# Second MLP's tiles 1 and 2: seven half-size block products for each two f-blocks

## The chip, the cores and the metric

The kernel runs on one core of one Trainium2 chip. The metric is device time in microseconds of one execution on that core, median of several runs. The kernel before takes 796.52 us (median of three: 794.61, 796.52, 796.79).

## What is computed

Clustered attention over 2 x 8 heads of 768 positions and 64 channels, and then two MLPs on the 1536 x 512 result. The change lies in the second MLP's first product, `x @ w_in`.

```python
def _moe_ref(x, w_in, w_out):            # first MLP, 512 -> 2048 -> 512
    h = x @ w_in
    g = h * np.cos(h)
    return (g @ w_out).astype(np.float32)

def _moe2_ref(x, w_in, w_out):           # second MLP, 512 -> 2048 -> 512
    h = x @ w_in
    g = np.where(h > 0.0, h, 1.0 * (np.exp(np.minimum(h, 0.0)) - 1.0))
    return (g @ w_out).astype(np.float32)
```

## The kernel before

The 1536 tokens are cut into three tiles of 512 (`t`), the 2048 inner columns into 16 f-blocks of 128 (`f`). `SEQ` lists the 96 steps (m, t, f): MLP m, tile t, block f. Every fp32 operand is held as two fp32r parts, a rounded high part and the rest (XH/XL of the activations in `X`, the two halves of a weight's slot, GH/GL of the inner result), and a product is three matmuls: high x high, high x low, low x high.

- `g1` (line 203) makes h of one step: 4 blocks of the contraction (kd) x 3 matmuls = 12 matmuls with 128 x 128 weights and 512 moving columns, summed in one PSUM bank (`ps_h`, 4 banks).
- `act` makes g of it: in the second MLP Relu and Exp on ACT (lines 236, 238), one operation on DVE (240), the copy GH (line 82 when on ACT) and the rest GL (245).
- `g2` (line 262) adds g's part of the output: 4 x 3 matmuls of 512 columns into four PSUM banks (`ps_a`), which stay for the 16 steps of a tile. `finish` copies them out at the tile's end.
- `x_hi`, `x_lo` (line 184) split a tile's x into XH, XL. `load_w` and `w_part` fetch the 16 slots of a MLP's weights and split them. For the second MLP the split goes on during its tile 0; tiles 1 and 2 only read the slots.

No engine's order is left to chance: every call goes into a list with a time in steps (tables `FIRST`, `PAIR`, `STEP`, ..., `LAST`, `MLP`), the list is sorted by it, and that is each engine's order of instructions. A step's `g1` in the second MLP stands at 1.6, its `g2` at 5.7, so `g2` runs about four steps behind. The table `OWN` and its like say which engine does an operation that several can do. `xpl` holds, in the attention stage, two kinds of buffers (R and xt, line 829 and 846) of three each.

Of the kernel before, what the change touches and what calls it, by code (L numbers as in the profile page):

```python
# [1015 lines left out]
```

## Time and profile before

| | |
|---|---|
| median of three runs | 796.52 us |
| the profiled execution, own time | 799.22 us |
| its span, first to last instruction | 797.4 us |
| TensorE matmul busy | 778.0 us (98%) |
| TensorE weight loads busy | 670.1 us (84%) |
| DVE, ACT, POOL busy | 507.9, 472.9, 329.3 us (64, 59, 41%) |
| granted TensorE clock, mean | 0.996 |

The attention stage takes the first 267 us, the first MLP goes to about 529 us, and the second MLP's three tiles take some 87 to 90 us each. A matmul's record (389 ns for 512 columns) is longer than the distance from one to the next, since matmuls are pipelined; it is the distance between starts that counts. Weight loads have records of their own (PEld) beside them. The records of the merged timeline give a start, the time to the end of the last instruction that they hold, and their number.

### The profile page before, as it was taken

The page shows a single profiled execution, that of the slowest core. Times are in us where ns is not written, and L with a number is a line of the kernel's source. Part 1 is how long each engine was busy: PE and PEld are TensorE (multiplying, and loading weights), DVE is VectorE, ACT ScalarE, POOL GpSimd, SP SyncE. Part 2 cuts the span into 40 slices and gives each one's busy share as a digit, 9 for nine tenths or more (in the row PEclk, how much of TensorE's full clock was granted, in tenths as well). Part 3 has the DMA queues.
Part 4 walks back from the last instruction along what each step waited for, and adds up shares of the span by engine and source line. Part 5 has one row for each costly group of instructions (what it writes and reads, how often), then busy time and mean ns, then how long its engine had stood idle before and what let it go on. Part 6 is the DMA issues. An engine that isn't in the chain of part 4 may idle for free.

```text
span 797.4 us, 11263 instructions
## 1 busy us (share of the span) xinstructions
PE 778.0 (98%) x4003; PEld 670.1 (84%) x4003; DVE 507.9 (64%) x791; ACT 472.9 (59%) x887; POOL 329.3 (41%) x419
## 2 busy tenths in 40 slices
PE   6999999999999999999999999999999999999998
PEld 5888998989898888888888888888888888888886
DVE  7899899999999999964545555997773111112110
ACT  5888998988989866743434434655452433334323
POOL 6666666766765633132321222256440122113211
PEclk9899999999999999999999999999999999999999
DMA  4637556548447395000000055643000100000001
GB/s 101 154 71 163 137 122 161 129 96 194 91 113 251 46 379 186 1 1 0 1 1 0 8 175 188 211 159 106 0 1 1 53 1 1 0 27 27 0 1 53
DMA packets 62919, 67.98 MB, mean 85 GB/s; under 512 B 30416, under 2 KB 51408, under 8 KB 62864
## 3 DMA queue, kind: packets, MB, share of 16 engines
q1 hardware_dynamic: 62864, 67.28, 30.2%
q8 instruction: 31, 0.51, 0.3%
q14 instruction: 24, 0.20, 0.1%
HBM read 46.17 MB, written 3.19 MB: 62 GB/s over the span
## 4 chain that ended last, share of the span: by engine, by line
PE 89%; DVE 7%; DMA 1%; ACT 1%; issue 0%; ACTq 0%
PE h L203 33%; PE a L262 33%; PE pt L774 7%; PE px L805 6%; PE s L751 4%; PE s L754 3%; PE pt_sim L586 2%; DVE m L759 2%; DVE PL L794 2%; DVE M L652 1%; PE pt_raw L445 1%; DMA row<-sum 1%; PE pt_mask L661 1%; ACT P L765 0%; DVE best L638 0%
## 5 line engine op out<-in xcount | busy, mean ns | idle before, releaser
L203 PE MATMUL h<-XH,slot 128*128 128x512 f32 x768 | 249.6, 389 | 0.0
L245 POOL TENSOR_TENSOR GL<-A,GH 128x512 fp32r<-128x512 f32 x77 | 104.3, 1355 | 285.4 <-ACT GH L82 275.3
L203 PEld LDWEIGHTS h<-XH,slot 128*128 128x128 f32 x768 | 144.2, 188 | 29.8
L203 PE MATMUL h<-XL,slot 128*128 128x512 f32 x384 | 149.4, 389 | 0.0
L262 PE MATMUL a<-GH,slot 128*128 128x512 f32 x384 | 124.2, 389 | 0.0
L240 DVE SCALAR_TENSOR_TENSOR A<-R,h 128x512 f32<-128x512 f32 x48 | 32.9, 685 | 136.7 <-ACT R L238 110.5
L262 PE MATMUL a<-slot,GH 128*128 128x512 f32 x384 | 118.1, 389 | 0.0
L794 DVE TENSOR_TENSOR PL<-pt,PH 128x384 fp32r<-128x384 f32 x192 | 99.8, 548 | 13.2 <-ACT PH L788 12.0
L759 DVE TENSOR_REDUCE m<-s 128x1 f32<-128x768 f32 x96 | 91.3, 951 | 3.0 <-PE s L754 2.8
L788 ACT ACTIVATE PH<-pt 128x384 fp32r<-128x384 f32 x192 | 84.0, 495 | 14.2 <-PE pt L774 13.9
L765 ACT ACTIVATE P<-s,m 128x768 f32<-128x768 f32 x96 | 87.2, 909 | 0.2
L262 PEld LDWEIGHTS a<-GH,slot 128*128 128x128 f32 x384 | 72.1, 188 | 15.1
L774 PE MATMUL pt<-ident,P 128*128 128x128 f32 x576 | 83.9, 280 | 0.8 <-DVE PL L794 0.8
L262 PEld LDWEIGHTS a<-slot,GH 128*128 128x128 f32 x384 | 72.1, 188 | 14.9
L203 PEld LDWEIGHTS h<-XL,slot 128*128 128x128 f32 x384 | 72.1, 188 | 14.8
L262 PE MATMUL a<-GL,slot 128*128 128x512 f32 x192 | 74.7, 389 | 0.0
L262 PE MATMUL a<-slot,GL 128*128 128x512 f32 x192 | 74.7, 389 | 0.0
L774 PEld LDWEIGHTS pt<-ident,P 128*128 128x128 f32 x576 | 66.8, 142 | 7.5 <-DVE PL L794 2.6
L82 ACT ACTIVATE GH<-A 128x512 fp32r<-128x512 f32 x74 | 46.5, 628 | 43.1 <-PE a L262 35.0
L236 ACT ACTIVATE R<-h 128x512 f32<-128x512 f32 x48 | 28.4, 593 | 67.8 <-PE h L203 59.3
L232 ACT ACTIVATE R<-R,cbias 128x512 f32<-128x512 f32 x48 | 34.8, 724 | 51.8 <-DVE R L229 51.5
L805 PE MATMUL px<-PH,V 128*128 128x384 f32 x192 | 63.8, 360 | 0.2 <-issue 0.2
(148 smaller groups left out, 1281.3 us busy)
## 6 DMA issues: line engine op xcount, KB each, us to landing
raw<-in_moe_w_in_dram SPq DMA_DIRECT2D x32, 512.0 KB, 4.9
raw<-in_moe_w_out_dram SPq DMA_DIRECT2D x32, 512.0 KB, 5.6
nat_k<-in_k_dram SPq DMA_DIRECT2D x16, 192.0 KB, 4.9
nat_q<-in_q_dram SPq DMA_DIRECT2D x16, 192.0 KB, 4.8
nat_v<-in_v_dram SPq DMA_DIRECT2D x8, 384.0 KB, 4.2
R<-row SPq DMA_DIRECT2D x32, 96.0 KB, 3.4
out_dram<-o SPq DMA_DIRECT2D x12, 256.0 KB, 2.0
X0k<-hi SPq DMA_DIRECT2D x7, 192.0 KB, 3.2
```

Source lines behind the costliest of these rows:

```text
L82: nc.scalar.activation(out=out, in_=in_, func=AF.Copy)
L203: nc.tensor.matmul(h, lhsT=a[:, kd, :], rhs=b, start=(kd == 0 and i == 0), stop=(kd == NKD - 1 and i == 2))
L232: nc.scalar.activation(out=R, in_=R, func=AF.Sin, scale=-2.0 * PI, bias=cbias[:, 1:2])
L240: nc.vector.scalar_tensor_tensor(out=A, in0=R, scalar=-1.0, in1=h, op0=ALU.add, op1=ALU.max)
L245: eng.tensor_tensor(out=GL, in0=A, in1=f32(GH), op=ALU.subtract)
L262: nc.tensor.matmul(accs[m, t][e], lhsT=a, rhs=b, start=(f == 0 and i == 0), stop=(f == NF - 1 and i == 2))
L759: nc.vector.tensor_reduce(out=m, in_=st[n]["s"][:, :, 0:HW], axis=AX.XY, op=ALU.max, negate=True)
L765: nc.scalar.activation(out=P, in_=st[n]["s"][:, :, 0:HW], func=AF.Exp, bias=st[n]["m"], accum_out=den_all[:, u % NDEN, j, r, 0:1])
L774: nc.tensor.transpose(pt[:, c * 128:(c + 1) * 128], st[n]["P"][:, e, c * 128:(c + 1) * 128], ident)
L788: nc.scalar.activation(out=ph, in_=pt, func=AF.Copy)
L794: nc.vector.tensor_tensor(out=pl, in0=pt, in1=f32(ph), op=ALU.subtract)
L805: nc.tensor.matmul(tx[g][:, 0:HW], lhsT=V2s[pp][:, j, c, :], rhs=halves[g][a][:, c, :], start=(n == 0), stop=(n == 2 * C - 1))
```

## The change

For tiles 1 and 2 of the second MLP, two f-blocks form a pair p (f = 2p and 2p+1). The weights of the pair are cut into four blocks of 256 contraction rows x 128 inner columns: A11, A12 are the two contraction halves of f = 2p+1, A21, A22 those of f = 2p. The tile's x is cut into four blocks of 256 contraction rows x 256 tokens, B11, B12, B21, B22. Instead of eight block products (24 matmuls of 512 columns for the pair) seven are formed, from sums of blocks: S1 to S4 of the A, T1 to T4 of the B. Each product (`prod`) is 2 contraction blocks x 3 matmuls of 256 columns, 42 matmuls for a pair, into half a PSUM bank.

- `s_u`, `s_one`, `s_two` add and split the S of each pair, S1 in tile 1 alone (it replaces A21 in the slot). S2 to S4 lie in one pair of tiles (`s_tiles`) that all pairs share.
- `b_sum`, `b_hi`, `b_lo` add and split the T and B once for each tile (table `WB`).
- `post` adds the products to the two blocks of h, in SBUF instead of PSUM; `act2` does what `act` did, from there.
- The table `WINO` orders all of it in pairs of steps. The tables `MLP` and `OWN` are new numbers throughout; the first copy of one head's keys (`HI2_ON['k', 1]`) goes from ACT to POOL; R and xt become slices of one tile `XR`, taken in turn by three as before, whose place the parts of B21, B22 and T2 take later.

```diff
@@ tables (MLP and OWN are replaced as a whole; the entries that the text speaks of) @@
-MLP = ({'g1': 1.9351, 'g2': 5.1777, 'load_w': 6.9247,
...
-        {'w_part:0': -2.691, 'g1': 1.6453, 'g2': 5.685, 'finish:0': 5.1595,
...
+MLP = ({'g1': 2.0325, 'g2': 5.796, 'load_w': 8.7032,
...
+        {'w_part:0': -1.5449, 'g1': 1.3739, 'g2': 5.8639, 'finish:0': 6.1734,
...
-OWN = {('whi', 0, 4): 'act', ('whi', 0, 5): 'pool',
...
+OWN = {('whi', 0, 4): 'dve', ('whi', 0, 5): 'dve',
...
+WINO = {'prod:0': 1.6, 'prod:1': 1.9725, 'prod:2': 2.6787, 'prod:3': 2.7425, 'prod:4': 2.7906, 'prod:5': 1.7613, 'prod:6': 3.234, 's_u:0': 0.9693, 's_u:1': 0.8845, 's_one:0': 1.3791, 's_one:1': 1.6966, 's_one:2': 2.1605, 's_two:0': 1.4297, 's_two:1': 1.5803, 's_two:2': 1.7361, 's_two:3': 2.1336, 's_two:4': 1.7614, 's_two:5': 2.2728, 'post:0': 2.7063, 'post:1': 2.7432, 'post:2': 3.0948, 'post:3': 3.2081, 'post:4': 3.2392, 'post:5': 3.6463, 'act2:0:0': 3.4126, 'act2:0:1': 3.4277, 'act2:0:2': 3.4505, 'act2:0:3': 3.4527, 'act2:0:4': 4.0437, 'act2:1:0': 4.1999, 'act2:1:1': 4.2131, 'act2:1:2': 4.3675, 'act2:1:3': 4.809, 'act2:1:4': 4.9979, 'g2:0': 4.8891, 'g2:1': 5.7143, 'finish:0': 6.1536, 'finish:1': 6.3053, 'finish:2': 6.3697, 'finish:3': 6.9415}
+WB = {1: {'b_sum:T3': -12.515, 'b_sum:T1': -8.3378, 'b_hi:B22': -12.3147, 'b_lo:B22': -8.8721, 'b_sum:T2': -4.6837, 'b_hi:B21': -10.5531, 'b_lo:B21': -10.0989, 'b_sum:T4': -0.1752, 'b_hi:T2': 0.3261, 'b_lo:T2': 0.3985, 'b_hi:B11': 0.0969, 'b_lo:B11': 1.4943, 'b_hi:T1': 0.9416, 'b_lo:T1': 2.25, 'b_hi:T3': 2.2503, 'b_lo:T3': 2.2727, 'b_hi:T4': 1.4624, 'b_lo:T4': 2.1361}, 2: {'b_sum:T3': -5.1851, 'b_sum:T1': -10.2681, 'b_sum:T2': -10.1178, 'b_sum:T4': -8.5532, 'b_hi:B11': 0.297, 'b_lo:B11': 0.439, 'b_hi:T2': 0.7126, 'b_lo:T2': 0.9837, 'b_hi:T1': 1.597, 'b_lo:T1': 2.1008, 'b_hi:T3': 0.7567, 'b_lo:T3': 1.2414, 'b_hi:T4': 0.9759, 'b_lo:T4': 1.6384, 'b_hi:B21': 0.5348, 'b_lo:B21': 1.5059, 'b_hi:B22': 2.4049, 'b_lo:B22': 2.6018}}
+BSUM_ON = "pool"
+B_ON = {"B11": ("act", "dve"), "B21": ("act", "pool"), "B22": ("act", "pool"), "T1": ("act", "dve"), "T2": ("act", "dve"),
+        "T3": ("act", "dve"), "T4": ("act", "dve")}
+SU_ON = ("pool", "pool")
+SONE_ON = "dve"
+G2_ON = (("act", "pool"), ("act", "pool"))
-HI2_ON = {('k', 0): 'act', ('k', 1): 'act', ('q', 0): 'act', ('q', 1): 'act'}
+HI2_ON = {('k', 0): 'act', ('k', 1): 'pool', ('q', 0): 'act', ('q', 1): 'act'}
...
-    xpl = ctx.enter_context(tc.tile_pool(name="xpl", bufs=2))
+    xpl = ctx.enter_context(tc.tile_pool(name="xpl", bufs=1))
+    XR = xpl.tile([128, 6, HW], F32, tag="xr", name="xr")
...
+    TH = TT // 2
+    PRODS = (("11", "B11", 0, 1), ("S2", "T2", 0, 0), ("S1", "T1", 1, 1), ("S3", "T3", 1, 0), ("22", "T4", 2, 0),
+             ("12", "B21", 3, 0), ("S4", "B22", 3, 1))
+    BT, BF, hw, HA = {}, {}, {}, {}
...
+    def b_tiles(t, b):
+
+        own = {"B11": 0, "T3": 1, "T4": 2, "T1": 3}
+        if b in own:
+            if (t, b) not in BT:
+                BT[t, b] = [blk(xs_pool[0].tile([128, TT], F32R, tag=f"{n}{own[b]}", name=n)) for n in ("XH", "XL")]
+        elif (1, b) not in BT:
+            u = xpl.tile([128, 9, TH], F32R, tag="xr", name="BX")
+            top = top_pool[0].tile([128, 2, TH], F32R, name="BY")
+            BT[1, "B22"] = [u[:, 0:2], u[:, 2:4]]
+            BT[1, "B21"] = [u[:, 4:6], u[:, 6:8]]
+            BT[1, "T2"] = [top, (u[:, 8], s_tiles()[0][:, 3])]
+        return BT[t, b] if b in own else BT[1, b]
...
+    def x_block(t, b):
+        i, j = int(b[1]) - 1, int(b[2]) - 1
+        return X[:, 2 * i:2 * i + 2, t * TT + j * TH:t * TT + (j + 1) * TH]
...
+    def b_sum(t, b):
+
+        a, c, op = {"T3": ("B22", "B12", ALU.subtract), "T1": ("B12", "B11", ALU.subtract),
+                    "T2": ("B22", "T1", ALU.subtract), "T4": ("B21", "T2", ALU.subtract)}[b]
+        if t > 1:
+            home = blk(X[:, ("T1", "T2", "T3", "T4").index(b), TT:2 * TT])
+        elif b == "T3":
+            home = blk(X[:, 2, 0:TT])
+        else:
+            home = x_block(t, {"T1": "B12", "T2": "B22", "T4": "B21"}[b])
+            need(*([("b_sum", t, "T3")] if b == "T1" else [("b_lo", t, {"T2": "B22", "T4": "B21"}[b])]))
+        for x in (a, c):
+            if x[0] == "T":
+                need(("b_sum", t, x))
+            else:
+                BF[t, x] = x_block(t, x)
+        eng = nc.vector if BSUM_ON == "dve" else nc.gpsimd
+        eng.tensor_tensor(out=home, in0=BF[t, a], in1=BF[t, c], op=op)
+        BF[t, b] = home
+        made("b_sum", t, b)
...
+    def b_hi(t, b):
+        if b[0] == "T":
+            need(("b_sum", t, b))
+        else:
+            BF[t, b] = x_block(t, b)
+        for o, x in pieces(b_tiles(t, b)[0], BF[t, b]):
+            copy_on(B_ON[b][0], o, x)
+        made("b_hi", t, b)
...
+    def b_lo(t, b):
+        need(("b_hi", t, b))
+        hi, lo = b_tiles(t, b)
+        eng = nc.vector if B_ON[b][1] == "dve" else nc.gpsimd
+        for k, (o, x) in enumerate(pieces(lo, BF[t, b])):
+            eng.tensor_tensor(out=o, in0=x, in1=f32(piece(hi, k) if isinstance(lo, tuple) else hi), op=ALU.subtract)
...
+    UV = X[:, 0:2, 0:TT].rearrange("p c (e n) -> p c e n", e=2)
+    HV = X[:, 2:4, 0:TT].rearrange("p c (e n) -> p c e n", e=2)
+
+    def s_u(t, p, i):
+
+        ih, il, _, _ = w_views(1, 2 * p + 1 - i)
+        eng = nc.vector if SU_ON[i] == "dve" else nc.gpsimd
+        eng.tensor_tensor(out=X[:, i, 0:TT].rearrange("p (k f) -> p k f", k=NKD), in0=f32(ih), in1=f32(il), op=ALU.add)
...
+    def s_one(p, i):
+
+        a = UV[:, 1, 0]
+        ih, il, _, _ = w_views(1, 2 * p)
+        eng = nc.vector if SONE_ON == "dve" else nc.gpsimd
+        if i == 0:
+            eng.tensor_tensor(out=a, in0=a, in1=UV[:, 1, 1], op=ALU.add)
+        elif i == 1:
+            copy_on("act", ih[:, 0:2], k2(a))
+        else:
+            eng.tensor_tensor(out=il[:, 0:2], in0=k2(a), in1=f32(ih[:, 0:2]), op=ALU.subtract)
...
+    def s_two(t, p, i):
+        hi, lo = s_tiles()
+        if i == 0:
+            nc.vector.tensor_tensor(out=UV[:, 0, 0], in0=UV[:, 1, 0], in1=UV[:, 0, 0], op=ALU.subtract)
+        elif i == 1:
+            nc.vector.tensor_tensor(out=UV[:, :, 1], in0=UV[:, :, 1],
+                                    in1=UV[:, 0:1, 0].to_broadcast([128, 2, TH]), op=ALU.subtract)
+        else:
+            x, ks = ((UV[:, 0], slice(0, 2)), (UV[:, 1, 1:2], slice(2, 3)))[i % 2]
+            if i < 4:
+                copy_on("act", hi[:, ks], x)
+            else:
+                nc.vector.tensor_tensor(out=lo[:, ks], in0=x, in1=f32(hi[:, ks]), op=ALU.subtract)
...
+    def a_block(t, p, a):
+        if a in ("S2", "S4", "S3"):
+            i = ("S2", "S4", "S3").index(a)
+            return [x[:, i].rearrange("p (k f) -> p k f", k=2) for x in s_tiles()]
+        ih, il, _, _ = w_views(1, 2 * p + 1 if a[0] == "1" else 2 * p)
+        ks = slice(0, 2) if a in ("11", "S1") else slice(2, 4)
+        return [ih[:, ks], il[:, ks]]
...
+    def prod(t, p, i):
+        a, b, bank, half = PRODS[i]
+        need(("b_lo", t, b))
+        if a[0] == "S":
+            need(("s_one", p, 2) if a == "S1" else ("s_two", t, p, 5 if a == "S3" else 4))
+        if (t, p, bank) not in hw:
+            hw[t, p, bank] = ps_h.tile([128, TT], F32, tag="h", name="h")
+        o = hw[t, p, bank][:, half * TH:(half + 1) * TH]
+        ah, al = a_block(t, p, a)
+        bh, bl = b_tiles(t, b)
+        for k in range(2):
+            for n, (x, y) in enumerate(((ah, bh), (ah, bl), (al, bh))):
+                nc.tensor.matmul(o, lhsT=x[:, k], rhs=piece(y, k), start=(k == 0 and n == 0), stop=(k == 1 and n == 2))
...
+    def post(t, p, i):
+        need(*[("prod", t, p, n) for n in ((0, 1), (0, 1), (2, 3), (2, 3), (4,), (5, 6))[i]])
+        hp = [hw.get((t, p, b)) for b in range(4)]
+        if i == 0:
+            HA[t, p] = [wk.tile([128, TT], F32, tag="A", name="A") for _ in range(2)]
+        A0, A1 = HA[t, p]
+        h2 = lambda x: x.rearrange("p (a n) -> p a n", a=2)
+        if i == 0:
+            nc.scalar.activation(out=HV[:, 0], in_=h2(hp[0]), func=AF.Copy)
+        elif i == 1:
+            nc.vector.tensor_tensor(out=HV[:, 0, 0], in0=HV[:, 0, 0], in1=HV[:, 0, 1], op=ALU.add)
+        elif i == 2:
+            nc.vector.tensor_tensor(out=HV[:, 1], in0=h2(hp[1]), in1=HV[:, 0, 0:1].to_broadcast([128, 2, TH]), op=ALU.add)
+        elif i == 3:
+            nc.vector.tensor_tensor(out=A0[:, TH:TT], in0=hp[1][:, TH:TT], in1=HV[:, 1, 0], op=ALU.add)
+        elif i == 4:
+            nc.vector.tensor_tensor(out=A0[:, 0:TH], in0=hp[2][:, 0:TH], in1=HV[:, 1, 0], op=ALU.add)
+        else:
+            nc.vector.tensor_tensor(out=h2(A1), in0=h2(hp[3]), in1=HV[:, :, 1], op=ALU.add)
+        made("post", t, p, i)
+
...
+    def act2(t, p, e, i):
+        if i == 0:
+            acts[1, t, f] = (HA[t, p][e], wk.tile([128, TT], F32, tag="R", name="R"),
+                             *(wk.tile([128, TT], F32R, tag=n, bufs=3, name=n) for n in ("GH", "GL")))
+        A, R, GH, GL = acts[1, t, f]
+        if i == 0:
+            nc.scalar.activation(out=R, in_=A, func=AF.Relu, scale=-1.0)
+        elif i == 1:
+            nc.scalar.activation(out=R, in_=R, func=AF.Exp, scale=-1.0)
+        elif i == 2:
+            nc.vector.scalar_tensor_tensor(out=A, in0=R, scalar=-1.0, in1=A, op0=ALU.add, op1=ALU.max)
+        elif i == 3:
+            copy_on(G2_ON[e][0], GH, A)
+        else:
+            eng = nc.vector if G2_ON[e][1] == "dve" else nc.gpsimd
+            eng.tensor_tensor(out=GL, in0=A, in1=f32(GH), op=ALU.subtract)
+        made("act", 1, t, f, i)
...
-            Rs[u] = xpl.tile([128, HW], F32, tag="R", bufs=3, name="R")
+            Rs[u] = XR[:, 3 + u % 3]
...
-                xts[u] = xpl.tile([128, HW], F32, tag="xt", bufs=3, name="xt")
+                xts[u] = XR[:, u % 3]
...
+            if m == 1 and t > 0:
+                for name, time in WINO.items():
+                    fn, own = named(name)
+                    if fn is finish:
+                        if f == NF - 1:
+                            at(t0 - 1 + time, fn, m, t, *own)
+                    elif f % 2 == 0:
+                        if fn is s_one:
+                            if t == 1:
+                                at(t0 + time, fn, f // 2, *own)
+                        elif fn is g2:
+                            at(t0 + time, fn, m, t, f + own[0])
+                        else:
+                            at(t0 + time, fn, t, f // 2, *own)
+                if f == 0:
+                    for name, time in WB[t].items():
+                        fn, own = named(name)
+                        at(t0 + time, fn, t, *own)
+                continue
```

## Rows read from the trace of the kernel before

**Rows 1.** The page: span, and busy time of each engine.

```profile
span 797.4 us, 11263 instructions
PE 778.0 (98%) x4003; PEld 670.1 (84%) x4003; DVE 507.9 (64%) x791; ACT 472.9 (59%) x887; POOL 329.3 (41%) x419
```

**Rows 2.** The page: the chain that ended last, share of the span by engine.

```profile
PE 89%; DVE 7%; DMA 1%; ACT 1%; issue 0%; ACTq 0%
```

**Rows 3.** Busy time by stage: first MLP, then tiles 0 and 1 of the second.

```profile
core 0: us, PE busy (x) PEld busy (x) DVE busy (x) ACT busy (x) POOL busy (x), PEclk, DMA share, GB/s
267.40:528.70 261.30, 261.30 (x1162) 217.03 (x1161) 182.36 (x223) 133.36 (x194) 75.11 (x59) 1.00 0.29 98
528.70:616.00 87.30, 87.30 (x387) 72.29 (x386) 59.01 (x68) 43.20 (x63) 37.08 (x25) 1.00 0.11 39
616.00:703.00 87.00, 87.00 (x385) 72.09 (x384) 13.76 (x21) 31.09 (x55) 19.44 (x15) 1.00 0.03 13
```

**Rows 4.** Timeline of PE inside tile 2, with 512-column matmuls.

```profile
703.26 0.39 PE L203 MATMUL h<-XL,slot 128*128 128x512 f32 x1
703.49 0.62 PE L203 MATMUL h<-XH,slot 128*128 128x512 f32 x2
703.94 0.39 PE L203 MATMUL h<-XL,slot 128*128 128x512 f32 x1
```

**Rows 5.** Timeline of PE, a run of 384-column matmuls.

```profile
275.42 0.34 PE L805 MATMUL px<-PL,V 128*128 128x384 f32 x1
...
275.94 0.34 PE L805 MATMUL px<-PH,V 128*128 128x384 f32 x1
```

**Rows 6.** Timeline of PE, a run of 32-column matmuls on 128-column weights.

```profile
70.05 0.26 PE L586 MATMUL pt_sim<-CC,X1q 128*128 128x32 f32 x1
...
70.38 0.26 PE L586 MATMUL pt_sim<-CC,X0q 128*128 128x32 f32 x1
```

**Rows 7.** Single lines: count, then duration in ns, least/median/most.

```profile
L245 POOL TENSOR_TENSOR GL<-A,GH x32: 1282/1296/1304, 630.5 to 786.0; 128x512 fp32r<-128x512 f32 x32
L82 ACT ACTIVATE GH<-A x32: 615/632/633, 629.7 to 785.3; 128x512 fp32r<-128x512 f32 x32
L240 DVE SCALAR_TENSOR_TENSOR A<-R,h x32: 678/689/690, 628.4 to 784.5; 128x512 f32<-128x512 f32 x32
L184 DVE TENSOR_TENSOR XL<-X,XH x20: 676/684/2883, 347.6 to 699.4; 128x512 fp32r<-128x512 f32 x20
```

**Rows 8.** Groups by line and shape (count, busy us, mean ns): narrower operations.

```profile
L621 DVE TENSOR_TENSOR sm<-sm,mx 128x192 f32<-128x192 f32 x2 | 0.7, 358 | 0.1
L794 DVE TENSOR_TENSOR PL<-pt,PH 128x384 fp32r<-128x384 f32 x192 | 99.8, 548 | 13.2 <-ACT PH L788 12.0
L422 ACT ACTIVATE CC<-pt_c 128x128 fp32r<-128x128 f32 x1 | 0.3, 277 | 0.0
L788 ACT ACTIVATE PH<-pt 128x384 fp32r<-128x384 f32 x192 | 84.0, 495 | 14.2 <-PE pt L774 13.9
L82 ACT ACTIVATE X1k<-T1k 64x768 fp32r<-64x768 f32 x1 | 0.8, 844 | 0.0
L86 POOL TENSOR_SCALAR XH<-X 128x512 fp32r<-128x512 f32 x8 | 6.8, 850 | 3.6 <-PE h L203 3.6
```

**Rows 9.** Timeline near the end: ACT, DVE, POOL, last matmul.

```profile
783.81 0.62 ACT L238 ACTIVATE R<-R 128x512 f32<-128x512 f32 x1
...
784.53 0.69 DVE L240 SCALAR_TENSOR_TENSOR A<-R,h 128x512 f32<-128x512 f32 x1 [4.75 <-ACT R L238]
...
785.32 0.63 ACT L82 ACTIVATE GH<-A 128x512 fp32r<-128x512 f32 x1 [0.88 <-PE a L262]
...
786.03 1.28 POOL L245 TENSOR_TENSOR GL<-A,GH 128x512 fp32r<-128x512 f32 x1 [0.74 <-ACT GH L82]
...
793.25 0.39 PE L262 MATMUL a<-slot,GL 128*128 128x512 f32 x1
```

**Rows 10.** DMA issues on the page: transfer, count, size, us to landing.

```profile
raw<-in_moe_w_in_dram SPq DMA_DIRECT2D x32, 512.0 KB, 4.9
```

More of the change, by code (lines that the diff above doesn't have):

```diff
@@ L110, in made @@
         did.add(key)
-    slots, raws, w_u, slot_pool = {}, {}, {}, {}
+    slots, raws, w_u, slot_pool, top_pool = {}, {}, {}, {}, []
     SEQ = [(m, t, f) for m in range(2) for t in range(NTT) for f in range(NF)]
@@ new lines, in s_tiles, with pieces, piece @@
+    def s_tiles():
+        if "s" not in BT:
+            BT["s"] = [wst.tile([128, 4, TH], F32R, tag="u", name="sums") for _ in range(2)]
+        return BT["s"]
+    def pieces(x, y):
+        return [(x[k], y[:, k]) for k in range(2)] if isinstance(x, tuple) else [(x, y)]
+    def piece(x, k):
+        return x[k] if isinstance(x, tuple) else x[:, k]
+    def x_block(t, b):
+        i, j = int(b[1]) - 1, int(b[2]) - 1
+        return X[:, 2 * i:2 * i + 2, t * TT + j * TH:t * TT + (j + 1) * TH]
@@ new lines, in blk @@
+    def blk(ap):
+        return ap.rearrange("p (k n) -> p k n", k=2)
+    def b_sum(t, b):
[17 more added lines that the diff above has]
+        made("b_sum", t, b)
@@ new lines, in b_hi @@
+    def b_hi(t, b):
[12 more added lines that the diff above has]
+            eng.tensor_tensor(out=o, in0=x, in1=f32(piece(hi, k) if isinstance(lo, tuple) else hi), op=ALU.subtract)
+        made("b_lo", t, b)
@@ new lines @@
+    UV = X[:, 0:2, 0:TT].rearrange("p c (e n) -> p c e n", e=2)
[4 more added lines that the diff above has]
+        eng.tensor_tensor(out=X[:, i, 0:TT].rearrange("p (k f) -> p k f", k=NKD), in0=f32(ih), in1=f32(il), op=ALU.add)
+        made("s_u", t, p, i)
+    def s_one(p, i):
+        need(("s_u", 1, p, 0), ("s_u", 1, p, 1), ("g1", 1, 0, 2 * p))
+        a = UV[:, 1, 0]
+        ih, il, _, _ = w_views(1, 2 * p)
+        k2 = lambda x: x.rearrange("p (k f) -> p k f", k=2)
+        eng = nc.vector if SONE_ON == "dve" else nc.gpsimd
[5 more added lines that the diff above has]
+            eng.tensor_tensor(out=il[:, 0:2], in0=k2(a), in1=f32(ih[:, 0:2]), op=ALU.subtract)
+        made("s_one", p, i)
@@ new lines, in s_two @@
+    def s_two(t, p, i):
+        if t == 1:
+            need(("s_one", p, 0))
+        need(("s_u", t, p, 0), ("s_u", t, p, 1))
+        hi, lo = s_tiles()
[10 more added lines that the diff above has]
+                nc.vector.tensor_tensor(out=lo[:, ks], in0=x, in1=f32(hi[:, ks]), op=ALU.subtract)
+        made("s_two", t, p, i)
@@ new lines, in a_block @@
+    def a_block(t, p, a):
[18 more added lines that the diff above has]
+                nc.tensor.matmul(o, lhsT=x[:, k], rhs=piece(y, k), start=(k == 0 and n == 0), stop=(k == 1 and n == 2))
+        made("prod", t, p, i)
+        if i == 6:
+            made("g1", 1, t, 2 * p)
+            made("g1", 1, t, 2 * p + 1)
@@ new lines, in act2 @@
+    def act2(t, p, e, i):
+        f = 2 * p + e
+        need(("post", t, p, 3 + e if e == 0 else 5), *([("act", 1, t, f, i - 1)] if i else []))
+        if i == 0:
[14 more added lines that the diff above has]
+        made("act", 1, t, f, i)
+        if i == 4:
+            for x in range(5, 8):
+                made("act", 1, t, f, x)
```

6 lines of the change are left out of this document (4 added, 2 removed).

## The prediction

> **What bounds the kernel now.** I read the page's busy shares first, then the chain of work that ended last, then a table by stage, then single matmul starts. The page gives PE 98% of a span of 797.4 us [rows 1], and the chain is PE for 89% [rows 2]. A share alone proves little, since matmul records overlap, so the stage table matters more: from 267.4 us on PE is busy in every microsecond, 261.30 of 261.30 in the first MLP and 87.00 of 87.00 in tile 1 of the second, at a granted clock of 1.00 (the 2.4 GHz level) [rows 3]. The starts then say what one matmul costs: the record at 703.49 holds two, so three matmuls of 512 columns lie between 703.26 and 703.94, 0.2267 us each [rows 4]; 87.00 us over the 384 matmuls of a tile is 0.2266 as well [rows 3]. So nothing waits in the MLPs, and the time of a stage there is a number of matmuls times a distance. In tile 1 the others have room: DVE 13.76, ACT 31.09, POOL 19.44 of 87 us [rows 3].
>
> **The change part by part.**
>
> **The matmuls.** Removed for each of 16 pairs (8 in tile 1, 8 in tile 2): 24 matmuls of 512 columns, 24 x 0.2267 = 5.44 us. Added: 42 matmuls of 256 columns. No matmul of that width is in the trace, so I bound its distance. 512 columns at 2.4 GHz are 213.3 ns, and the row has 226.7, 13.4 more; 384 columns are 160 ns, and three distances between 275.42 and 275.94 (two rows of the same kind left out between) are 173 each [rows 5], 13 more. One column per cycle and a constant of 13.4 thus describe both, and 256 columns give 106.7 + 13.4 = 120 ns. Below, each matmul must load its own 128 columns of weights: with only 32 moving columns the distance is still 0.33/3 = 110 ns [rows 6]. Above, a 256-column matmul should not be slower than a 384-column one with the same load, 173 ns. I take 120, the line through the two nearest widths, since it lies above the load's 110. The pair is then 42 x 0.120 = 5.04 us, 0.40 saved, 16 x 0.40 = **6.4 us**. At 110 it would be 4.62 and 13.1 us saved; at 173 it would be 7.27 and 29 us lost. The break-even is 5.44/42 = 129.5 ns, so the whole case hangs on ten nanoseconds: an eighth less arithmetic is bought with three quarters more instructions.
>
> By rows, load and columns do overlap: one after the other, 384 columns would take 110 + 160 = 270 ns, not 173 [rows 5, 6]. The Trainium skill speaks on the same point (TensorE: Matmul & The Clock Gate, Back-to-back issue gap): it says that the spacing in a stream of load and matmul pairs is set by both operations, and gives N/2.4 + 2.5 ns for the matmul by itself, 109 ns at 256 columns. Its formula would be 216 ns at 512, where this trace has 226.7 [rows 4], so the measurement decides; by the page's 109 the pair would be 4.6 us and the saving some 14 us.
>
> **The sums, on DVE, ACT and POOL.** Widths of 512 have rows: DVE 0.69, ACT 0.63, POOL 1.30 us [rows 7]. For 256, DVE lies between 358 ns at 192 and 548 at 384, by line 0.42; ACT between 277 at 128 and 495 at 384, 0.39 [rows 8].
> - DVE for a pair: six of 512 (two in `s_two`, two in `post`, two in `act2`), five of 256: 6 x 0.69 + 5 x 0.42 = 6.2 us; in tile 1 two of 256 more (`s_one`), 7.1. Before: 13.76/8 = 1.7.
> - ACT: eight of 512 (one in `s_two`, one in `post`, six in `act2`) and one of 256, in tile 1 two: at most 8 x 0.63 + 2 x 0.39 = 5.8. Before 3.9.
> - POOL: two `s_u` and two GL, 4 x 1.30 = 5.2. Before 2.4.
> - PE for a pair with its two `g2`: 5.04 + 24 x 0.2267 = 10.48.
>
> All lie beside PE, with 3.4 us left on DVE, the fullest. Cost taken: 0; if the cover goes, what counts is not the sums but the chain in front of one product.
>
> **The new waits.** By `WINO`, PE's order in a pair is product 0, odd `g2` of two pairs ago, products 5, 1, 2, 3, 4, even `g2` of the pair before, product 6. The tightest wait: S2 to S4 have one buffer, so `s_two`'s copy on ACT waits for product 6 of the pair before; behind it on ACT stand Relu and Exp of that pair's odd block. Then copy 0.63 and rest on DVE 0.69 with three handovers of 0.1 (ACT ends 784.43, DVE starts 784.53; DVE ends 785.22, ACT starts 785.32 [rows 9]) are 1.6 us, in which PE has product 0, a `g2` and product 5: 0.72 + 2.72 + 0.72 = 4.16. 2.5 us are left, 1.1 if two more DVE operations of 0.69 (`post` 5, `s_two` 1) stand ahead. `post` frees each PSUM bank before the next pair's product wants it: bank 0, read after product 1, is wanted again after three more products, a `g2` and product 6, 5.6 us later, against one ACT copy of 0.63. POOL's `s_u` waits for `s_two`'s last read, and GL of the odd block is queued behind it; that GL is wanted only in the odd `g2` of two pairs on. `g2` itself: after product 6, `post` 0.69, Relu 0.63, Exp 0.62, DVE 0.69, GH 0.63, GL 1.28 and six handovers of 0.1 are 5.1 us, against 11 us within a tile and two `g2`, 5.44, at the very end. Cost taken: 0 everywhere; bounds 0 to 1 us for the end, where 0.3 is left.
>
> **Between tiles.** For each tile ACT gets seven copies, DVE about 4 x 0.69 + 2 x 0.42 = 3.6 us, POOL two rests and four sums, 6 x 1.30 = 7.8. For tile 1 POOL's fall into tile 0, where it is busy 37.08 of 87.30 [rows 3]. Around the start of tile 2 DVE has 7.1 + 6.2 + 3.6 = 16.9 of two pairs' 20.96 us. Cost 0; if a product there waits, once, under 1 us.
>
> **The rest.** The first MLP is ordered anew; PE has no gap there [rows 3], so this can lose and not win: 0, with up to 6 us (a gain as large as mine) as the far end. `load_w` of the second MLP goes out 1.8 steps later and is used 1.1 steps later; between the two there stay 5.8 steps of 5.44, 31 us, on SP with no other traffic of weights, against 4.9 us to landing [rows 10]: 0. The start's one key copy leaves ACT (0.84) for POOL, at the 850 ns of 512 elements about 1.3 for 768 [rows 8]: taken 0, between -0.8 and +1.3. R and xt turn by three as before: 0. No DMA is added.
>
> **Sum.** The profiled execution's own time is 799.2 us, 1.8 more than its span. 799.2 - 6.4 = 792.8. It stands 2.7 us above the median of the runs, 796.5, so the median becomes 796.5 - 6.4 = **790.1 us**.
>
> **The rivals.**
> - The load's floor: the 13.4 ns are not paid at 256 columns, and the distance falls towards 110. Then up to 13.1 us, 783.4. For it: 32 columns reach 110 [rows 6]. Against it: both wider kinds pay the constant. The gap that the Trainium skill gives, cited above, would land here too. Chance 0.13.
> - Loads not hidden (slower): at 256 columns a load and a matmul last about as long, 107 to 110, and any part of one that can't lie under the other shows. It decides from 129.5 ns; half-way from 120 to 173 it is 146, 42 x 0.146 = 6.13, +0.69 x 16 = +11, 807. For it: no row has both full at once, a weight load's busy time grows from 72.09 of 87 towards all of it [rows 3]. Against it: at 384 no part shows. Chance 0.10.
> - A wait in each pair (slower): if the chain for S2 or the T2 of a tile takes more than the 4.16 us, PE waits in every pair; 1 us beyond it costs 16, less 6.4, 806. For it: DVE's line goes from 1.7 to 7 us a pair. Against it: at least 1.1 us left. Chance 0.07.
> - The gain is made and given back: the new order leaves PE gaps in the first MLP or at the tiles' starts, 3 to 7 us together, 793 to 797. Chance 0.15.
>
> **How the numbers follow.** The forecast, distances of 117 to 124 ns and at most 1 us of waits, is 788 to 793 and has 0.55. About 0.3%, 2.4 us, is what a measurement here can tell from no change. Faster: 0.55 + 0.13 + 0.03 of the last case = 0.71. Same: 0.12, the rest of it. Slower: 0.10 + 0.07 = 0.17. The range runs from 783 (the floor) to 797 (all given back) and leaves out the slower cases, 0.17.
>
> **What would show it.** Right: starts 120 ns apart inside a product, tiles 1 and 2 of some 84 us each with PE busy throughout, DVE between 50 and 60 us in each. Wrong at the first step: another distance. Wrong at the waits: idle time of PE released by DVE's rest of S or T. Wrong in the rest: PE below 261.3 of the first MLP's stretch, or that stretch longer.

## The result

The changed kernel takes **789.0 us** (median of six runs, 788.7 to 789.3) against 795.9 of the kernel before, measured beside it: a ratio of 0.9914, interval 0.9901 to 0.9927, 6.9 us faster. The forecast was 790.1, with a saving of 6.4.

The page of the changed kernel, its span and busy times (beside [rows 1]):

```profile
span 787.0 us, 12179 instructions
...
PE 770.1 (98%) x4291; PEld 675.7 (86%) x4291; DVE 616.5 (78%) x957; ACT 503.9 (64%) x948; POOL 401.1 (51%) x462
```

PE stays at 98%, and DVE and POOL rise by 109 and 72 us: the sums. By stage (columns as in [rows 3]), tile 1 lies in the third row, tile 2 in the fourth, up to the last matmul at 783.3:

```profile
263.40:524.00 260.60, 260.60 (x1159) 216.37 (x1158) 180.91 (x218) 130.26 (x192) 83.48 (x62) 1.00 0.28 97
524.00:611.00 87.00, 87.00 (x401) 72.69 (x400) 75.53 (x82) 47.95 (x70) 48.95 (x30) 1.00 0.12 42
611.00:700.00 89.00, 89.00 (x554) 80.25 (x554) 70.02 (x114) 49.32 (x92) 52.52 (x37) 1.00 0.04 13
700.00:784.00 84.00, 83.25 (x508) 74.30 (x506) 49.27 (x80) 43.62 (x77) 39.76 (x30) 1.00 0.05 19
```

PE is busy in all of these stretches but the last 0.7 us, so here too almost nothing waits (one wait of 0.2 us, below); the matmuls became cheaper in sum. The chain that ended last runs through nothing but PE in tile 2 (start, us, line, matmuls), and one turn of a pair goes from 742.95 to 753.42:

```profile
742.95 1.43 PE h L416 x12
744.38 2.75 PE a L271 x12
747.12 3.55 PE h L416 x30
750.67 2.75 PE a L271 x12
753.42 1.43 PE h L416 x12
```

That is 10.47 us a pair, the 10.48 of the prediction; all eight pairs of tile 2 keep it but the third, 10.67. From the first matmul of the first MLP to the end of the last one of the second it was 526.2 us (267.45 to 793.64) and is 519.9 (263.33 to 783.26): 6.3 saved. The spans themselves differ by 10.4, since the profiled execution of the kernel before reached the first MLP some 4 us later. It had a stretch with a granted clock of 0.86 on the way, but that doesn't explain the delay by itself: a second profile of the same kernel (run before_again, below) has 0.86 too, only earlier, and its first MLP starts at 262.52. Its MLPs take 526.2 again (to 788.74). All rows are of the kernel before, the first of the first profile:

```profile
24.00:48.00 24.00, 22.44 (x141) 20.28 (x140) 20.81 (x39) 18.32 (x41) 15.67 (x30) 0.86 0.63 145
```

```profile
0.00:24.00 24.00, 16.12 (x85) 13.25 (x85) 19.41 (x56) 15.76 (x28) 15.53 (x63) 0.86 0.40 100
24.00:48.00 24.00, 23.18 (x161) 20.73 (x161) 22.53 (x44) 21.76 (x48) 16.52 (x31) 1.00 0.62 142
```

### The profile page after: what moved, and what is told of

Same layout as the page of the kernel before. It is cut to its first block, busy times and chain, and to the rows that moved or that the text cites. A ratio compares the mean times of both kernels' runs of the same rounds, so it can differ in the third digit from the quotient of the medians.

```text
span 787.0 us, 12179 instructions
## 1 busy us (share of the span) xinstructions
PE 770.1 (98%) x4291; PEld 675.7 (86%) x4291; DVE 616.5 (78%) x957; ACT 503.9 (64%) x948; POOL 401.1 (51%) x462
## 4 chain that ended last, share of the span: by engine, by line
PE 89%; DVE 6%; DMA 3%; POOL 1%; SPq 0%; issue 0%; ACT 0%; POOLq 0%
PE a L271 33%; PE h L212 22%; PE h L416 10%; PE pt L975 7%; PE px L1006 6%; PE s L952 4%; PE s L955 3%; DVE m L960 2%; PE pt_sim L787 2%; DVE PL L995 1%; PE pt_raw L646 1%; DMA raw<-in_moe_w_out_dram 1%; DMA row<-sum 1%; DVE M L853 1%; DMA nat_q<-in_q_dram 1%; PE pt_mask L862 1%
## 5 line engine op out<-in xcount | busy, mean ns | idle before, releaser
L212 PE MATMUL h<-XH,slot 128*128 128x512 f32 x512 | 166.2, 389 | 0.0
L254 POOL TENSOR_TENSOR GL<-A,GH 128x512 fp32r<-128x512 f32 x46 | 66.6, 1447 | 145.4 <-ACT GH L90 115.2
L212 PEld LDWEIGHTS h<-XH,slot 128*128 128x128 f32 x512 | 96.1, 188 | 19.8
L212 PE MATMUL h<-XL,slot 128*128 128x512 f32 x256 | 99.6, 389 | 0.0
L989 ACT ACTIVATE PH<-pt 128x384 fp32r<-128x384 f32 x192 | 84.1, 495 | 12.9 <-PE pt L975 12.7
L271 PEld LDWEIGHTS a<-slot,GH 128*128 128x128 f32 x384 | 69.9, 188 | 12.8
L461 POOL TENSOR_TENSOR GL<-A,GH 128x512 fp32r<-128x512 f32 x32 | 42.3, 1320 | 60.2 <-ACT GH L90 51.9
L229 ACT ACTIVATE A<-h,cbias 128x512 f32<-128x512 f32 x48 | 32.8, 684 | 48.4 <-PE h L212 44.6
L233 DVE SCALAR_TENSOR_TENSOR R<-A,h 128x512 f32<-128x512 f32 x48 | 32.8, 683 | 38.8 <-ACT A L229 38.8
```

The costliest lines, as they stand in the source:

```text
L212: nc.tensor.matmul(h, lhsT=a[:, kd, :], rhs=b, start=(kd == 0 and i == 0), stop=(kd == NKD - 1 and i == 2))
L254: eng.tensor_tensor(out=GL, in0=A, in1=f32(GH), op=ALU.subtract)
L271: nc.tensor.matmul(accs[m, t][e], lhsT=a, rhs=b, start=(f == 0 and i == 0), stop=(f == NF - 1 and i == 2))
L461: eng.tensor_tensor(out=GL, in0=A, in1=f32(GH), op=ALU.subtract)
L989: nc.scalar.activation(out=ph, in_=pt, func=AF.Copy)
```

## The experiments

Theory A: the time moved by the number of matmuls times a distance of one column a cycle and 13.3 ns, and everything else is hidden. Rivals: B, narrow matmuls run at the weight load's 110 ns; C, part of the gain is the new order elsewhere; D, loads show beside 256 columns; E, the chains of sums have hardly any cover left.

**The distance by itself.** The kernel before, with the moving columns of the second MLP's first product in tiles 1 and 2 cut, and no sums:

```diff
+        w = 256 if m == 1 and t > 0 else TT        # 128 in split128
+        for c in range(0, TT, w):
...
-                nc.tensor.matmul(h, lhsT=a[:, kd, :], rhs=b,
+                    nc.tensor.matmul(h[:, c:c + w], lhsT=a[:, kd, :], rhs=b[:, c:c + w],
```

> The kernel before, with each 512-column matmul of the second MLP's first product in tiles 1 and 2 cut into two of 256 columns: 768 matmuls where 384 were, no sums, no other operation. Theory A (a matmul costs one column a cycle and 13.3 ns, 120 ns at 256 columns): 768 x 0.120 - 384 x 0.2267 = +5.1 us, about 801. Rival B (the constant is not paid at 256 columns, the distance is the weight load's 110 ns): 768 x 0.110 - 87.0 = -2.6 us, about 793. Rival D (loads not hidden beside 256 columns, 146 ns): +25 us, 821.

> The same with four matmuls of 128 columns for each of 512: 1536 matmuls. If the weight load of 110 ns is a floor under every matmul: 1536 x 0.110 - 87.0 = +82 us, about 878. If only columns and the constant count (53.3 + 13.3 = 66.7 ns): +15 us, about 811.

split256 took 800.7 us, 1.0057 of the kernel before (1.0033 to 1.0081); split128 took 879.4 (a single run). PE's timeline of split256, then of split128 (start, us, then the instruction). Three more matmuls stand between the two rows of each; the first row of split128 holds two:

```profile
702.72 0.28 PE L205 MATMUL h<-XH,slot 128*128 128x256 f32 x1
...
703.20 0.28 PE L205 MATMUL h<-XL,slot 128*128 128x256 f32 x1
```

```profile
702.91 0.39 PE L205 MATMUL h<-XH,slot 128*128 128x128 f32 x2
...
703.47 0.28 PE L205 MATMUL h<-XL,slot 128*128 128x128 f32 x1
```

Four distances at 256 columns from 702.72 to 703.20, 0.120 each; five at 128 from 702.91 to 703.47, 0.112. Theory A's 120 holds at 256 columns. At 128, where it would give 66.7, the distance is 112, near the 110 of the 32-column rows [rows 6]: the load's floor. So the larger of the two counts. B and D fall.

**The rest of the change alone.** The changed kernel with all of tiles 1 and 2 formed as before:

```diff
-            if m == 1 and t > 0:
+            if m == 1 and t > 2:
```

> The changed kernel with tiles 1 and 2 of the second MLP formed as before (eight block products): what is left of the change is the new order and places of work elsewhere, the key copy on POOL and the one tile for R and xt. Theory A (all of the gain is the matmuls' count): the time of before, 796 within 1. Rival C (part of the gain is the new order): 789 to 793.

> The kernel before, unchanged, for a second profile. In the first one the granted clock was 0.86 from 24 to 48 us and the first MLP started at 267.45 us, against 263.33 in the changed kernel. If that stretch is the run and not the kernel, the first MLP starts here at 263 to 265 us and the span from there to the last matmul is 526.2 again.

classic_tables took 796.6 us, 1.0019 (1.0004 to 1.0035): no gain, and 0.3 to 2.8 us lost. Its MLPs take 526.2 us like those of the kernel before. In the profile what is lost stands at the end: ACT copies the last results out from 788.92 on, and the four issues to memory begin at 789.54, when the matmuls end; in the changed kernel they begin at 781.88, 1.4 us before the last matmul's end. From the last matmul's end to the end of the span it is 5.0 us here (789.56 to 794.6) and 3.7 in the changed kernel (783.26 to 787.0), 1.3 more. The likely reason is that the old form uses times for `finish` that were meant for another place; the changed kernel doesn't run them there. before_again took 794.3 in its single run, and its first MLP starts at 262.52, just ahead of the 263 to 265 expected. C falls. SP's queue in the timeline, of classic_tables and then of the changed kernel:

```profile
789.54 1.81 SPq L484 DMA_DIRECT2D out_dram<-o  x4
```

```profile
781.88 2.37 SPq L484 DMA_DIRECT2D out_dram<-o  x4
```

**One tile alone.** Seven products in tile 2 only (`t > 1`, and S1 is made in tile 2):

```diff
-            if m == 1 and t > 0:
+            if m == 1 and t > 1:
...
-                            if t == 1:
+                            if t == 2:
                                 at(t0 + time, fn, f // 2, *own)
```

> The changed kernel with the seven products in tile 2 alone; tile 1 as before. Theory A: 8 pairs x 0.40 = 3.2 us saved, 792.7. Rival C (the gain comes from elsewhere): 789. A wait at the change from tile 1's to tile 2's form would add to it once, under 2 us.

It took 794.5 us, 0.9994 (0.9980 to 1.0009), which can't be told from the kernel before and lies within the 792.7 and up to 2 us more that theory A allowed. The traces show more than the median: the pairs turn in 10.47 us, so 3.2 are saved, the MLPs take 524.4 us (264.15 to 788.59) against 526.2, 1.8 less, and so some 1.5 are lost at the change of form. Half of that is lost here, in PE's timeline, where a product waits for DVE (0.60 is the idle time):

```profile
697.54 0.39 PE L271 MATMUL a<-slot,GL 128*128 128x512 f32 x1
698.53 0.38 PE L416 MATMUL h<-XH,slot 128*128 128x256 f32 x1 [0.60 <-DVE A L249]
```

So by the traces of the MLPs half of the change gives half of the gain, less its entry. The medians alone don't show it: 794.5 is 2.1 below classic_tables, but that kernel also loses the 1.3 us at its end.

**The cover of the sums.** The copy of S2 and S4 on ACT three, five and seven times, so that the tightest chain grows by 1.26, 2.52 and 3.78 us by the durations of [rows 7]:

```diff
             if i < 4:
-                copy_on("act", hi[:, ks], x)
+                for _ in range(3 if i == 2 else 1):        # 5, 7
+                    copy_on("act", hi[:, ks], x)
```

> The changed kernel with the ACT copy of S2 and S4 done three times in each pair, so that the chain from product 6 to the next pair's product 1 is 2 x 0.63 = 1.26 us longer. The trace of the changed kernel has the rest of S2 ready about 2.4 us before product 1 starts. Theory A (all of the sums lie beside PE): no change, 789 within 0.5. Rival E (the chain's cover is nearly used up): up to 16 x 1.26 = +20 us.

> The same copy five times, 2.52 us longer. Theory A with 2.4 us of room: 0.1 to 0.3 us of wait in each pair, +2 to +5 us, 791 to 794.

> The same copy seven times, 3.78 us longer. Theory A with 2.4 us of room: 1.3 to 1.5 us of wait in each of 16 pairs, +21 to +24 us, 810 to 813; ACT then has about 9.6 of a pair's 11.9 us, so it is the chain and not ACT's own sum that sets it.

They took **797.5, 819.0 and 842.3** us, 8.5, 30 and 53 above the changed kernel. Theory A's times failed in all three. s_copy_x3 is within rival E's "up to 20", but not as a fixed price for each pair, as the turns below show.

The room of 2.4 us, from which these expectations were made, is not in the changed kernel's trace. In a wide view DVE's record at 744.51 holds two operations in 1.60 us; the first of them, the rest of S2 and S4, takes 1.27 us beside POOL's GL, where 0.69 is usual, and ends at 745.78. That leaves 1.9 us before product 1 (timelines of the changed kernel, tile 2's sixth pair, then its first, DVE's rest before product 1 in each):

```profile
744.51 1.27 DVE L393 TENSOR_TENSOR sums<-X,sums 128x512 fp32r<-128x512 f32 x1
...
747.67 0.28 PE L416 MATMUL h<-BY,sums 128*128 128x256 f32 x1
```

```profile
743.93 1.30 POOL L461 TENSOR_TENSOR GL<-A,GH 128x512 fp32r<-128x512 f32 x1 [3.32 <-ACT GH L90]
```

```profile
693.88 1.11 DVE L393 TENSOR_TENSOR sums<-X,sums 128x512 fp32r<-128x512 f32 x1
...
695.11 0.28 PE L416 MATMUL h<-BY,sums 128*128 128x256 f32 x1
```

By the same two records 13 of the 16 pairs have 1.2 to 1.9 us. The first three of tile 2 have 0.1 (the last two rows), 0.4 and nothing: in the third the rest ends at 716.34 and product 1 starts at 716.06, so its first matmul that reads the rest has to wait, the 0.2 us of that pair. E holds in part: these three have hardly any cover, the others have.

The starts of one product in each pair give the turn of the pairs:

| kernel | a usual pair of tile 1 | into tile 2 | last four of tile 2 | time |
|---|---|---|---|---|
| changed | 10.47 | 10.47 | 10.47 | 789.0 |
| s_copy_x3 | 10.47 | 16.6 | 10.87 | 797.5 |
| s_copy_x5 | 11.7 | 17.4 | 12.2 | 819.0 |
| s_copy_x7 | 13.0 | 18.7 | 13.5 | 842.3 |
| x3_su_dve | 11.3 | 13.0 | 11.1 | 805.4 |
| x5_su_dve | 12.7 | 14.4 | 12.4 | 825.9 |
| x3_su_late | 12.0 | 16.9 | 10.5 | 809.2 |
| x5_su_late | 13.4 | 17.1 | 11.85 | 832.0 |

In all of the rows below s_copy_x3 single pairs in both tiles turn more slowly still, up to 16.8 us apart from the turn into tile 2, so a usual pair alone doesn't give the time.

Two things make up most of s_copy_x3's 8.5 us. From 718 us to the last pair of tile 2 the chain that ended last has no PE left in it: it is a ring that closes through the queues of ACT and DVE alone. One turn, from line 438 to line 438:

```profile
740.22 0.42 DVE A L438
...
741.00 0.64 ACT R L453
...
741.67 0.64 ACT R L455
...
742.34 0.70 DVE A L457
...
743.12 0.58 ACT GH L90
...
743.74 0.64 ACT sums L90
744.41 0.64 ACT sums L90
745.07 0.94 ACT sums L90 x2
746.01 0.53 ACT R L453
746.57 0.64 ACT R L455
...
747.23 1.52 DVE A L457
748.75 1.44 DVE X L434
...
750.29 0.70 DVE X L436
...
751.08 0.42 DVE A L438
```

`post`, Relu and Exp of the even block, `act2` on DVE, GH, the S copies, Relu and Exp of the odd block, `act2` (line 457), `post` 1 (434), `post` 2 (436): each waits for the one before, some by data and some only because it stands behind in its queue. 10.87 us, and each pair of copies more adds 1.28: 12.15 and 13.43 by sum, 12.2 and 13.5 measured. Two steps of it are too long. Line 457 takes 1.52 us where it took 0.69 at 742.34, and 434 takes 1.44 where a 256-column addition takes 0.42. Beside both stood POOL's two additions of weight parts (POOL's timeline of s_copy_x3):

```profile
746.91 2.99 POOL L359 TENSOR_TENSOR X<-slot 128x512 f32<-128x512 f32 x2 [1.78 <-DVE sums L394]
```

Without those 1.85 us the ring would be 9.0 with three copies and 7.8 in the changed kernel, an estimate from these durations, 2.7 below PE's 10.47. The delayed chain pushes DVE's work into the time of POOL's, and the delay grows. The timelines of the changed kernel show the same operations for the same pair, DVE's two first, then POOL's:

```profile
746.04 0.68 DVE L456 SCALAR_TENSOR_TENSOR A<-R,A 128x512 f32<-128x512 f32 x1
749.22 0.42 DVE L433 TENSOR_TENSOR X<-X 128x256 f32<-128x256 f32 x1 [2.50 <-ACT X L431]
```

```profile
746.26 2.86 POOL L359 TENSOR_TENSOR X<-slot 128x512 f32<-128x512 f32 x2 [1.03 <-DVE sums L393]
```

The first starts 0.22 us ahead of POOL's 2.86 us and keeps its 0.68; the second starts 0.10 after their end. The Trainium skill (SBUF — State Buffer, Who interferes with whom) says that a DVE instruction with two inputs in SBUF contends with a GpSimd instruction that reads SBUF, for an exclusive lock, and that one with at most one input in SBUF, outside of the two-port modes, does not contend. The traces agree: 1.52 for 0.69 beside POOL, and line 436, with an input in PSUM, took 0.69 at 750.29 beside POOL's GL (749.87 to 751.3).

Such meetings also stand in the changed kernel, without any copy added, and PE's turn of 10.47 covers them there. The same 256-column addition (line 433 there) has a median of 0.67 us over its 16 pairs, the longer ones mostly in tile 1, and took 1.51 at 620.79 beside POOL's additions from 618.71 to 622.03 (count, then least/median/most in ns):

```profile
L433 DVE TENSOR_TENSOR X<-X x16: 424/670/1512, 608.1 to 770.2; 128x256 f32<-128x256 f32 x16
```

The other part is one wait at the start of tile 2, where the changed kernel had 0.1 us of room, and the clock behind it (columns as in [rows 3]; the clock is the third from the right):

```profile
697.30:700.70 3.40, 0.34 (x3) 0.14 (x2) 2.08 (x5) 2.97 (x6) 1.54 (x1) 0.86 0.00 0
700.70:706.30 5.60, 5.58 (x24) 5.36 (x25) 4.18 (x7) 3.06 (x6) 3.55 (x3) 0.50 0.00 0
```

After 3.1 us of waiting for ACT's copies the granted clock is 0.50, the lower of the two levels, for 5.6 us, and 24 matmuls of 256 columns take 5.6 us instead of 2.9. The turn is 16.6 in place of 10.47, 6.1 more: 3.1 of waiting, 2.7 of slow matmuls and some tenths around them. With 0.4 for each of the last five pairs and 1.0 in two pairs of tile 1 that is 9.1, less the 0.2 of the third pair, which is not lost here: 8.9, against 8.5 by the medians.

**Away from POOL.** With the copy three and five times, POOL's additions were put on DVE (first two lines of the diff), and in a second pair of runs left on POOL but put behind its GL of the odd block (last two lines). Theory F says that DVE was held up by POOL, rival G that the two queues are simply full:

```diff
-SU_ON = ("pool", "pool")
+SU_ON = ("dve", "dve")
...
-'s_u:0': 0.9693, 's_u:1': 0.8845, 's_one:0': 1.3791, 's_two:0': 1.4297,
+'s_u:0': 1.01, 's_u:1': 1.0, 's_one:0': 1.451, 's_two:0': 1.452,
```

> The kernel with the copy of S2 and S4 three times (797.5 us), and the pair's two additions of the weights' parts (s_u) on DVE instead of POOL. In that kernel's trace PE follows a ring of ACT and DVE work of 10.87 us a pair, in which two DVE operations with both inputs in SBUF took 1.52 and 1.44 us beside POOL's s_u, where they take 0.69 and 0.42 otherwise. Theory F (DVE was held up by POOL): the ring loses 1.85 us and gains the two additions, 2 x 0.69, between post 1 and post 2: 10.87 - 1.85 + 1.38 = 10.40, below PE's 10.48, so 789 to 791, although DVE does 1.4 us more in each pair. Rival G (the two queues are simply full): 16 x 1.38 on top, 819.

> The same with the copy five times (819.0 us with s_u on POOL). Theory F: the ring is 10.40 + 1.28 = 11.68, 1.2 above PE's 10.48, so 789 + 16 x 1.2 = 808. Rival G: 819 + 22 = 841.

> The kernel with the copy of S2 and S4 three times (797.5 us), with POOL's two s_u of the next pair moved behind the odd block's GL in POOL's queue (and s_one 0 and s_two 0, which read them, behind the even block's act2 on DVE). With s_u on DVE the odd act2 and post 1 fell back to 0.69 and 0.42 us, but the second s_u was held up by POOL's GL of the odd block, 1 us. Here, by the same durations, s_u runs beside post 2 to 4, which have an input in PSUM, and no DVE operation with both inputs in SBUF meets POOL at work. Theory F (those are held up, the others not): the ring is 10.87 - 1.85 = 9.0 us, PE is the bound again, 789 to 790. Rival G (the queues are full): no better than 797.

> The same with the copy five times (819.0 us without the move). Theory F: the ring is 10.3 by itself, but the odd block's GL comes later, s_u ends some 1 us after the even block's act2 wants to start and holds it up by 1 to 1.5 us: 11.3 to 11.8 a pair, 802 to 810. Rival G: 819.

The four took 805.4, 825.9, 809.2 and 832.0 us. F's times failed in all four. G's fit only x3_su_late, where it said no more than "no better than 797"; x3_su_dve and x5_su_dve lie between the two, and x5_su_late above both. In tile 2 the turns tell why. In x3_su_dve lines 457 and 434 are back at 0.69 and 0.42, but the two additions that came to DVE (line 359) take 2.38 instead of 1.38, since the second meets POOL's GL (timeline of x3_su_dve, all engines):

```profile
753.08 0.69 DVE L457 SCALAR_TENSOR_TENSOR A<-R,A 128x512 f32<-128x512 f32 x1 [0.46 <-ACT R L455]
...
753.75 0.42 DVE L434 TENSOR_TENSOR X<-X 128x256 f32<-128x256 f32 x1
...
754.09 2.38 DVE L359 TENSOR_TENSOR X<-slot 128x512 f32<-128x512 f32 x2
...
754.57 1.36 POOL L462 TENSOR_TENSOR GL<-A,GH 128x512 fp32r<-128x512 f32 x1 [3.58 <-ACT GH L90]
```

With the additions late (x3_su_late) tile 2's pairs turn in 10.51, and the chain is PE's alone again, as theory F said and as full queues would not give:

```profile
742.30 1.43 PE h L417 x12
...
752.81 1.43 PE h L417 x12
```

With five copies F gave 11.3 to 11.8 a pair, and 11.85 is measured in tile 2's last four. But in tile 1, where S1 is made as well, the move puts the sums that follow the additions into the ring, and two DVE operations of it are held up (1.46 and 1.69 us for 0.69), the first beside POOL's additions (677.33 to 679.87), the second beside its GL (681.16 to 682.45), with PE waiting again:

```profile
678.96 1.46 DVE A L457
...
681.32 1.69 DVE X L386
...
685.85 2.16 PE h L417 x16
```

So that POOL holds DVE up is shown by where the long operations appear and vanish; none of these runs is without such a meeting, and that three copies would then be free in both tiles stays open.

## Why the prediction was right

- **The distance** was the step on which all hung, and it held: 120 ns forecast from the 384- and 512-column rows [rows 4, 5], 120 in split256. In the changed kernel itself the records stand 118 to 119 apart inside the products, and part of the difference comes back in the next `g2`, which takes 2.75 us in place of 12 x 0.2267 = 2.72. In PE's timeline four distances lie between 748.39 and 748.86:

```profile
748.39 0.28 PE L416 MATMUL h<-XH,slot 128*128 128x256 f32 x1
...
748.63 0.40 PE L416 MATMUL h<-XH,slot 128*128 128x256 f32 x2
748.86 0.28 PE L416 MATMUL h<-XL,slot 128*128 128x256 f32 x1
```

  The pair is at 10.47. The count for a pair, not the distance inside a product, is the number to trust.
- **The floor.** It was named at 110 ns from 32 columns [rows 6] and is 112 at 128. The formula of the Trainium skill (TensorE: Matmul & The Clock Gate, Back-to-back issue gap) gives 109 ns for 256 columns; no run here shows that, and the measured 120 decides.
- **The sums at no cost** held in the kernel as it is: PE's chain is unbroken in tile 2, one wait of about 0.2 us stands in its third pair (forecast, for its start: once, under 1 us), and none at the end (forecast 0 to 1). But the sums were sized too small: DVE is busy 70.0 us in the 89 of tile 1's row, 66 for 84 us, and not 50 to 60; in tile 2's row it is 49.3. The forecast took each operation at its length alone, and beside POOL many are longer.
- **The rest at no cost** held: classic_tables.
- **The profiled execution and the median.** The sum was made against 799.2 and carried over to the median, and that was needed: 3.3 us of that execution were its own.
- **What failed** is the reason given for the third rival's low chance. "At least 1.1 us left" was counted along one chain, with each operation at its length alone. In the changed kernel 13 pairs have that much, and the first three of tile 2 have 0.4 us or less. The margin of the ring through the in-order queues was not worked out, and not the price of DVE and POOL meeting: 1.26 us added, less than most pairs have, cost 8.5 us. That no more than 0.2 us was lost at those three pairs was luck: no term of the prediction put the room there so low.
- **Open.** The MLPs' traces give 6.3 us and the medians 6.9. The start of the first MLP lies between 261.4 and 264.8 us in all the profiles but the first one of the kernel before (267.45), so 0.6 is within what the stage ahead of it varies by, but it was not traced further. Of the 1.1 us between the forecast 790.1 and 789.0, 0.6 is the reference: the kernel before had a median of 796.5 at first and of 795.9 with the later runs.

## What to carry to other kernels

Where PE is busy throughout, price a rewritten product by instructions times distance, and take the distance as the larger of the weight load's distance and one column a cycle plus a constant, with both from rows of the trace at the same granted clock. An eighth of the arithmetic came down to 7% of the pair's first product, since the 13.3 ns are paid 42 times and not 24. To say that work beside PE is free, follow a full turn of each in-order queue, not one chain, and look for DVE operations with both inputs in SBUF that a delay would push beside POOL's.

## What the runs showed of the hardware

- A wait can cost more than itself: in s_copy_x3, after 3.1 us without matmuls, TensorE ran 5.6 us at a granted clock of 0.50, which nearly doubled the loss (5.8 us).
- Held up by POOL, a DVE addition of 256 columns took 1.44 us instead of 0.42, more than three times; the 512-column operation beside it took 1.52 instead of 0.69, little more than twice.
- At 256 columns a weight load (110 to 112 ns, the distance where it is the floor) and a matmul's columns (106.7 ns at 2.4 GHz) are nearly equal, and the distance is 120 ns, the same 13 ns above the columns as at 384 and 512: nothing of the load shows.
